# Threshold attention and a gated MLP on one core: for two of 32 head pairs, thresholds are subtracted by TensorE

## The chip, the cores and the metric

The kernel runs on one core of a Trainium2 chip. The metric is the device time of one execution in microseconds (us); the kernel before has a median of 1337.23 us over three runs (1337.0 to 1337.47). The engines of the core are called PE (TensorE), ACT (ScalarE), DVE (VectorE), POOL (GpSimd) and SP (SyncE).

## What is computed

```
q, k, v: (8, 8, 576, 64) float32        # batch, heads, sequence, head dim
scores = q @ k.T / 8
thresh = max(scores, last axis) - tau   # tau = 0.02
scores = where(scores >= thresh, scores, -1e9)
attn   = softmax(scores)                # sum + 1e-9
x      = (attn @ v) as (4608, 512)      # tokens by heads * head dim
h      = x @ w_in                       # 512 x 2048
out    = (h * sigmoid(1.702 * h)) @ w_out   # 2048 x 512
```

Everything is float32. The weights arrive as 64-bit floats and are converted on the chip.

## The kernel before

**Attention.** Two heads of a batch make a pair, so there are 32 pairs n, and four pairs make a batch of 576 tokens. Scores are kept transposed, keys on partitions: a pair has nine key tiles j of 64 keys (NK = 9), and a PSUM tile holds, for one j, both heads h and the two halves c of the queries, each in its own 64x64 quarter of the PE array. Two key tiles make an SBUF tile t of 128 x 1152 (four of them and a short last one of 576, so NKT = 4). The steps of a pair, with their line in the profile:

- load_qk and load_v (L356, L367): DMAs issued by SP; prep (L467): two DVE transposes, one each for q and k.
- scores_run (L483): PE, four matmuls of 64x288 for each j, into one of three PSUM places (psA).
- keep (L500): ACT copies the place to SBUF, 128 x 576, and frees it.
- in_groups (L506): DVE takes maxima per tile t through a transposing reduction; over_tiles (L515) and over_halves (L526, L530) finish the maximum of each query, less the threshold gap. over_halves joins the two key halves in four pieces of 32 partitions and then one step over all 128.
- The thresholds are spread over all partitions into a tile mb: by spread_max (L541), one DVE transpose, for pair 2 and from pair 8 on; for pairs 0, 1 and 3 to 7 (BY_DMA) by turn_rows (L536, L537), row_out (L550) and row_in (L559): DVE turns the row, SP sends it to DRAM and reads it back to 64 partitions at a time.
- sub (L564): DVE subtracts mb from the scores in place, five instructions a pair.
- mask (L570): ACT, Prelu with a slope of 1e30 for negative values, so that they become hugely negative; exps (L574): ACT, Exp.
- sums_by_pe and values (both L585): PE matmuls of the weights by ones (den) and by v (pv). Pairs 0 to 4 have their sums from PE (BY_PE = 5), later ones from DVE.
- one_row (L616), spread_sums (L640, L642) and place_x (L659): DVE makes the reciprocals and writes x, transposed, into the xT tiles.

Pairs 1 and 3 have their scores and transposed inputs in an area of their own (APART), which later serves the feed-forward.

**Weights.** load_w (POOL queue, L418, L419) brings 32 pieces of a weight, which DVE (cv_ex, cv_frac, cv_end: L429, L443, L447, L455) and ACT (cv_power, L437) convert. Pieces wait in two places in the arena and in four staging places inside w_out.

**Feed-forward.** The tokens are taken in 18 blocks of 256. The first two go through mm1_0 (PE, L714), tanh (ACT, L683), gelu_0 (DVE, L720) and mm2 (L696); later ones through mm1 (L674) or, for the last four, product1 (L779), and through product (L865), seven products in place of eight. mm1_0 of the first two blocks needs place_x of pairs 0 to 3, that is the whole first batch.

**What sets the order.** No queue order is written by hand. Each step is entered by task(...) with an engine, a cost in us, a rank, what it comes after, and the places that it takes and gives back. run_in_order then plays the tasks through with these costs: whenever an engine is free, it takes the ready task with the lowest rank whose places are free, and issues its instructions at that moment, so the play decides the order of each engine's queue. The rank of an attention step is its pair number plus a bias by the step's name, from EARLY for pairs 0 to 3, SECOND for pairs 4 to 7 and LATER for the rest; weights have ranks of their own (CV, W_RANK). On the chip each queue runs in that order and waits on semaphores.

Of the kernel before, what the change touches and what calls it, by code (L numbers as in the profile page):

```python
# [10 lines left out]
FP32 = mybir.dt.float32  # L11
# [8 lines left out]
P = 128  # L20
# [10 lines left out]
def kernel(  # L31
# [83 lines left out]
    stop = const.tile([P, 1], FP32, name="stop")  # L115
    shift = const.tile([P, 1], FP32, name="shift")
# [9 lines left out]
    for x in ("raw0", "raw1", "qkT0", "qkT1", "mb"):  # L126
# [6 lines left out]
        "exps": -13.03,  # L133
        "in_groups": 3.54,
        "keep": 8.7,
        "load_qk": -0.35,
        "load_v": 3.02,
        "mask": -4.3,
        "one_group": -16.49,
        "one_row": 10.29,  # L140
        "over_halves": 4.51,
        "over_tiles": -2.08,
        "place_x": -19.47,
        "prep": -10.76,
        "row_in": 6.33,
        "row_out": 13.15,
        "scores_run": 17.81,
        "spread_max": -2.62,
        "spread_sums": 6.57,
        "sub": 6.26,  # L150
        "sums_by_pe": 0.52,
        "turn_rows": -2.02,
        "values": 6.25,
        "w_sum": 2.08,
        "x_sum": -12.81,
    }
    SECOND = {
        "exps": -9.22,
        "in_groups": 17.42,
        "keep": 18.09,  # L160
        "load_qk": -6.19,
        "load_v": 2.25,
        "mask": -4.66,
        "one_group": 1.4,
        "one_row": -7.39,
        "over_halves": -5.63,
        "over_tiles": -0.54,
        "place_x": -17.43,
        "prep": 1.16,
        "row_in": -11.07,  # L170
        "row_out": -10.78,
        "scores_run": -2.82,
        "spread_max": 8.98,
        "spread_sums": 4.05,
        "sub": 6.07,
        "sums_by_pe": 26.56,
        "turn_rows": -2.56,
        "values": 3.27,
        "w_sum": -0.95,
        "x_sum": 0.01,  # L180
    }
    LATER = {
        "exps": 3.18,
        "in_groups": 6.02,
        "keep": 0.05,
        "load_qk": -5.33,
        "load_v": 3.86,
        "mask": 11.98,
        "one_group": -4.73,
        "one_row": -15.77,  # L190
        "over_halves": 0.98,
        "over_tiles": 0.3,
        "place_x": 4.38,
        "prep": 4.34,
        "row_in": 6.22,
        "row_out": 6.41,
        "scores_run": -12.36,
        "spread_max": -11.89,
        "spread_sums": -3.87,
        "sub": -1.6,  # L200
        "sums_by_pe": -3.04,
        "turn_rows": 14.13,
        "values": -6.55,
        "w_sum": 4.92,
        "x_sum": 4.0,
    }
    CV = {
        "cv_end": -9.13,
        "cv_ex": 4.45,
        "cv_frac": 2.56,  # L210
        "cv_power": -3.6,
        "load_w": -6.63,
# [4 lines left out]
    QUARTERS = ("scores", "scores_run", "values", "sums_by_pe")  # L217
# [76 lines left out]
    JOINT = 7  # L294

# [183 lines left out]
    def scores(n, j):  # L479
        ps = psA.tile([P, 2, 512], FP32, name="ps", tag="ps")  # L480
        for h in range(2):
            for c in range(2):
                nc.tensor.matmul(  # L483
                    ps[ts(c, KT), h, 0:SH],
                    lhsT=mats[n, 1][ts(h, D), ts(j, KT)], rhs=mats[n, 0][ts(h, D), ts(c, SH)],
                    start=True, stop=True,
                )
        if j == NK - 1:
            del mats[n, 0], mats[n, 1]
        pss[n, j] = ps  # L490
# [31 lines left out]
    def over_halves(n):  # L522
        r = stats[n, ALU.max]
        o = work.tile([P, QB], FP32, name="fold", tag="fold", bufs=1)
        for x in range(4):
            nc.vector.tensor_scalar(  # L526
                out=o[ts(x ^ 1, 32)], in0=r[ts(x, 32)], scalar1=gap[ts(x, 32)], scalar2=None,
                op0=ALU.subtract,
            )
        nc.vector.scalar_tensor_tensor(  # L530
            out=r, in0=r, scalar=gap, in1=o, op0=ALU.subtract, op1=ALU.max
        )

    def turn_rows(n):

        nc.vector.tensor_copy(out=flat[0][:, 0:QB], in_=stats[n, ALU.max])  # L536
        nc.vector.transpose(out=flat[1], in_=flat[0])  # L537

# [52 lines left out]
    def values(n, tiles):  # L591
        if 0 in tiles:
            pvs[n] = psA.tile([P, 2, 512], FP32, name="pv", tag="ps")
        v_m, pv = vs[n], pvs[n]
        by_values(n, lambda j, h: v_m[:, j, h, :], [pv[:, c, :] for c in range(2)], tiles)
        if n < NPAIR:
            free_scores(n, tiles)
# [304 lines left out]
    nc.gpsimd.memset(ones, 1.0)  # L902
    nc.gpsimd.dma_start(
# [26 lines left out]
    BY_PE = 5  # L930
# [7 lines left out]
    W_RANK = (16.81, 18.37, 9.14, 15.61, 0.39, 3.55)  # L938
# [211 lines left out]
    for n in range(NP):  # L1150
# [65 lines left out]
        else:  # L1216
            for js in [range(x, x + 3) for x in range(0, NK, 3)] if n >= WHOLE else [[x] for x in range(NK)]:
                new = sum((own(n, "s_m") if x < NK - 1 else ("s_t",) for x in js if x % 2 == 0), ())
                a = task(
                    "PE", 0.484 * slow * len(js), r, scores_run, n, js, after=[pq, pk] + after,  # L1220
                    take=("psA",) * len(js) + new,
                    give=own(n, "qkT0", "qkT1") if js[-1] == NK - 1 else (),
                )
                after = [a]
                for j in js:
                    copied(n, r, j, a)
        a = task("DVE", 0.35, r, over_tiles, n, ALU.max, after=mx)
        a = task("DVE", 1.05, r, over_halves, n, after=[a, tau_done])
        if n in BY_DMA:
            a = task("DVE", 0.4, r, turn_rows, n, after=[a], take=("row",))  # L1230
            a = task("SP", 0.6, r, row_out, n, after=[a], lag=3.3)
            m = task(
                "SP", 1.0, r, row_in, n, after=[a], take=own(n, "mb"), give=("row",),
                lag=5.2,
            )
        else:
            m = task("DVE", 0.78, r, spread_max, n, after=[a], take=own(n, "mb"))
        spread[n] = m
        ws, subs = [], [m]
        for t in range(NKT + 1):  # L1240
            tail = t == NKT
            a = task(
# [9 lines left out]
        if n < NPAIR:  # L1252

            pv = den = None
            for t in every:
                first = t == 0
                den = task(
                    "PE", (0.97 if t < NKT else 0.484) * slow, r, sums_by_pe, n, [t], True, after=[ws[t], den],
                    take=("psM", "psM") if first else (),
                )  # L1260
                pv = task(
                    "PE", (0.97 if t < NKT else 0.484) * slow, r, values, n, [t], after=[ws[t], den, pv, lv],
                    take=("psA",) if first else (), give=(back[t],) if t < NKT else ("s_t", v_m),
                )
            su = []
            a = task("DVE", 1.07, r, one_row, n, after=[den], give=("psM", "psM"))
        else:
# [3 lines left out]
            if n < BY_PE:  # L1271
                a = task("PE", 4.36, r, sums_by_pe, n, every, False, after=ws + [pv], take=("psA",), give=back)
                a = task("DVE", 1.07, r, one_row, n, after=[a], give=("psA",))
            else:
                su = [
                    task("DVE", 0.66 if t == NKT else 1.27, r, in_groups, n, t, ALU.add, after=[ws[t]])
                    for t in range(NKT + 1)
                ]
                a = task("DVE", 0.35, r, over_tiles, n, ALU.add, after=su + [pv], give=back)
                a = task("DVE", 1.6, r, one_group, n, after=[a])  # L1280
# [40 lines left out]
```

## Time and profile before

| What | Value |
|---|---|
| median of three runs | 1337.23 us |
| profiled execution, its own time | 1339.0 us |
| its span, first to last instruction | 1337.1 us |
| mean granted PE clock | 0.981 |
| PE busy | 1268.7 us (95%) |
| DVE busy | 1051.7 us (79%) |
| ACT busy | 646.0 us (48%) |
| POOL busy | 246.7 us (18%) |
| shares of the chain that ended last | PE 57%, DVE 26%, ACT 7%, issue 4%, DMA 4% |

The page of the profile cuts the span in 40 slices and gives the busy share of each engine in tenths. Groups of instructions are given by line, engine and operation, with the shape written and read, the count, busy time and mean of one. A float32 matmul of the program leaves two records, so the counts of PE in the profile are twice those of the code: 36 matmuls of scores for a pair are 72 records. The view of waits puts a wait down to the event that came last; the chain follows the work that ended last back from the end of the span; the timeline lists instructions in order of time, with the idle time ahead of them in brackets.

### The profile page before, as it was taken

What the parts mean: (1) busy time and instruction counts of PE and PEld (TensorE: products, weight loads), DVE (VectorE), ACT (ScalarE), POOL (GpSimd) and SP (SyncE); (2) the same over time, 40 slices, a digit from 0 to 9 for tenths busy, and PEclk for the clock granted to TensorE, in tenths of its full rate; (3) what the DMA queues carried; (4) which work ended last, traced back from release to release, by engine and by line L of the source; (5) the groups of instructions that cost most, each with busy time, mean ns of one, the idle gap of its engine ahead of it and who ended that gap; (6) DMA issues with size and microseconds to landing.
All of it is one profiled execution on the core that took longest, in us unless ns stands there. A gap on an engine that the chain in (4) does not pass through costs nothing.

```text
span 1337.1 us, 22553 instructions
## 1 busy us (share of the span) xinstructions
PE 1268.7 (95%) x9128; PEld 983.2 (74%) x9128; DVE 1051.7 (79%) x1720; ACT 646.0 (48%) x830; POOL 246.7 (18%) x290
## 2 busy tenths in 40 slices
PE   5739899899999999999999999999999999999998
PEld 2426774357777777777878777777777778888887
DVE  7899899899999888878788888878787892662642
ACT  4885473866565545555455554454555540210210
POOL 1012111002122120302121202121121216120120
PEclk8869999899999999999999999999999999999999
DMA  8597875545221212111212121211211010000000
GB/s 157 178 240 212 248 222 132 90 93 86 46 42 36 52 37 52 27 44 21 51 36 52 36 52 37 52 37 27 51 29 34 19 34 0 17 1 24 9 0 32
DMA packets 245473, 88.48 MB, mean 66 GB/s; under 512 B 229626, under 2 KB 233722, under 8 KB 245370
## 3 DMA queue, kind: packets, MB, share of 16 engines
q1 hardware_dynamic: 231642, 49.02, 18.4%
q0 software_dynamic: 11360, 37.74, 9.5%
q8 instruction: 71, 1.16, 0.3%
q10 hardware_dynamic: 2368, 0.30, 0.2%
q14 instruction: 32, 0.26, 0.1%
HBM read 73.36 MB, written 9.47 MB: 62 GB/s over the span
## 4 chain that ended last, share of the span: by engine, by line
PE 57%; DVE 26%; ACT 7%; issue 4%; DMA 4%; SPq 2%; DVEq 0%; ACTq 0%
PE ops L865 22%; PE hps L674 10%; PE pv L585 7%; PE ps L483 6%; DVE part L506 6%; DVE arena L564 6%; PE ps L779 4%; PE ps L865 4%; ACT arena L574 3%; PE ops L779 3%; DVE arena L686 2%; ACT arena L570 2%; DVE fold L526 2%; DVE arena L467 2%; ACT arena L500 1%
## 5 line engine op out<-in xcount | busy, mean ns | idle before, releaser
L506 DVE TRANSPOSE_TENSOR_REDUCE part<-arena 128x36 f32<-128x1152 f32 (+1 forms) x295 | 359.9, 1239 | 92.9 <-ACT arena L500 83.5
L674 PE MATMUL hps<-xT,w_in 128*128 128x256 f32 x1536 | 339.7, 381 | 2.7 <-DVE arena L686 2.6
L674 PEld LDWEIGHTS hps<-xT,w_in 128*128 128x128 f32 x1536 | 290.4, 190 | 51.0 <-DVE arena L686 7.0
L500 ACT COPY arena<-ps 128x576 f32<-128x576 f32 x288 | 171.2, 645 | 174.2 <-PE ps L483 174.1
L570 ACT ACTIVATE arena<-arena 128x1152 f32<-128x1152 f32 (+1 forms) x160 | 169.3, 1058 | 153.2 <-DVE arena L564 153.2
L483 PE MATMUL ps<-arena 64*64 64x288 f32 x2304 | 178.7, 424 | 41.1 <-ACT arena L574 16.8
L865 PE MATMUL ops<-w_out,arena 128*128 128x256 f32 x896 | 203.5, 382 | 4.0 <-DVE arena L686 4.0
L564 DVE TENSOR_TENSOR arena<-arena 128x1152 f32<-128x1152 f32 (+1 forms) x158 | 196.4, 1290 | 8.2 <-DMA arena<-row 7.7
L574 ACT ACTIVATE arena<-arena,shift,scl 128x1152 f32<-128x1152 f32 (+1 forms) x160 | 200.3, 1252 | 4.2
L865 PEld LDWEIGHTS ops<-w_out,arena 128*128 128x128 f32 x896 | 169.3, 190 | 32.6 <-DVE arena L686 7.8
L831 POOL TENSOR_TENSOR arena<-arena 128x256 f32<-128x256 f32 x56 | 51.9, 927 | 650.4 <-DVE arena L686 541.2
L483 PEld LDWEIGHTS ps<-arena 64*64 64x64 f32 x2304 | 86.9, 139 | 108.4 <-ACT arena L500 30.9
L585 PE MATMUL pv<-arena 64*64 64x288 f32 x2176 | 160.5, 409 | 0.0
L865 PE MATMUL ops<-arena 128*128 128x256 f32 x672 | 150.8, 381 | 0.0
L865 PEld LDWEIGHTS ops<-arena 128*128 128x128 f32 x672 | 127.5, 190 | 19.2 <-issue 2.2
L683 ACT ACTIVATE th<-hps 128x512 f32<-128x512 f32 x112 | 65.9, 588 | 134.3 <-PE hps L674 107.8
L585 PEld LDWEIGHTS pv<-arena 64*64 64x64 f32 x2176 | 82.6, 134 | 54.2 <-issue 12.5
L887 DVE SCALAR_TENSOR_TENSOR osb<-ops,osb 128x256 f32<-128x256 f32 x98 | 39.3, 413 | 59.1 <-PE ops L865 55.9
L686 DVE SCALAR_TENSOR_TENSOR arena<-th,hps 128x512 f32<-128x512 f32 x96 | 64.0, 667 | 24.0 <-ACT th L683 23.4
L714 PE MATMUL hps<-xT,w_in 128*128 128x256 f32 x256 | 58.6, 390 | 3.6 <-DVE arena L720 3.6
L714 PEld LDWEIGHTS hps<-xT,w_in 128*128 128x128 f32 x256 | 49.2, 195 | 13.1 <-DVE arena L720 4.4
L844 POOL TENSOR_TENSOR arena<-arena 128x512 f32<-128x512 f32 x28 | 35.6, 1270 | 115.1 <-PE ops L865 115.1
(110 smaller groups left out, 1107.3 us busy)
## 6 DMA issues: line engine op xcount, KB each, us to landing
arena<-in_v_dram SPq DMA_DIRECT2D x128, 144.0 KB, 3.3
arena<-in_q_dram SPq DMA_DIRECT2D x128, 72.0 KB, 3.1
out_dram<-osb SPq DMA_DIRECT2D x36, 256.0 KB, 2.0
arena<-in_k_dram SPq DMA_DIRECT2D x124, 72.0 KB, 2.5
w_out<-in_moe_w_in_dram POOLq DMA_DIRECT2D x12, 512.0 KB, 7.7
arena<-in_moe_w_out_dram POOLq DMA_DIRECT2D x12, 512.0 KB, 5.4
w_out<-in_moe_w_in_dram POOLq DMA_DIRECT2D x12, 511.6 KB, 9.3
arena<-in_moe_w_out_dram POOLq DMA_DIRECT2D x12, 511.6 KB, 6.2
```

The lines of the kernel that those rows point to most:

```text
L483: nc.tensor.matmul(ps[ts(c, KT), h, 0:SH], lhsT=mats[n, 1][ts(h, D), ts(j, KT)], rhs=mats[n, 0][ts(h, D), ts(c, SH)], start=True, stop=True,)
L500: nc.scalar.copy(out=sT[n, t][:, u], in_=pss.pop((n, j))[:, :, 0:SH])
L506: nc.vector.tensor_reduce(out=stats[n, op][:, t * 2 * QB : min(2 * t + 2, NK) * QB], in_=sT[n, t].rearrange("p u h (g d) -> p (u h g) d", ...
L564: nc.vector.tensor_tensor(out=s, in0=s, in1=mbs[n].unsqueeze(1).to_broadcast(list(s.shape)), op=ALU.subtract)
L570: nc.scalar.activation(out=s, in_=s, func=AF.Prelu, alpha=STEEP)
L574: nc.scalar.activation(out=s, in_=s, func=AF.Exp, scale=scl, bias=shift)
L585: nc.tensor.matmul(o[c][ts(h, D), 0:SH], lhsT=left(j, h)[ts(c, KT)], rhs=sT[n, t][ts(c, KT), u, h, :], start=(j == 0), stop=(j == NK - 1),)
L674: nc.tensor.matmul(hidden[j][:, ts(f, BLK)], lhsT=w_in[:, c, ds((f * HF + j) * P, P)], rhs=xTs[blk][:, c, :], start=(c == 0), stop=(c == N ...
L686: nc.vector.scalar_tensor_tensor(out=g[:, :, j, :], in0=two(ths.pop(j)), scalar=1.0, in1=two(hidden.pop(j)), op0=ALU.add, op1=ALU.mult,)
L714: nc.tensor.matmul(hidden[j][:, ts(i, BLK)], lhsT=w_in[:, c, ts(j, P)], rhs=xTs[i][:, c, :], start=(c == 0), stop=(c == NDC - 1),)
L779: nc.tensor.matmul(places[j, x], lhsT=left[:, c, ts(j, P)], rhs=right[:, c, :], start=(c == 0), stop=(c == 1),)
L865: nc.tensor.matmul(banks[blk][k][:, ts(o, HM)], lhsT=left[:, j, :], rhs=right[:, j, :], start=(j == 0), stop=(j == HF - 1),)
```

## The change

For the third and fourth pair (n = 2 and 3, TWICE) the subtraction on DVE goes. Their scores are computed, copied and reduced to maxima as before. over_halves then writes the thresholds straight into a small tile, in four pieces of 32 partitions in place of one step over 128 (and turn_rows' copy is not needed), and row_blocks transposes that tile and multiplies it by a constant pattern of ones and zeros (own_row), which gives, for each head, a block-diagonal arrangement of the thresholds, 128 x 288. again computes each key tile's scores a second time into PSUM and adds, in the same accumulation, four matmuls of a constant matrix of zeros and minus ones (minus) by that arrangement, so that PSUM holds scores less thresholds. mask_one applies Prelu to PSUM, one key tile at a time, and writes SBUF, over the first copy of the scores; exps runs as before. Pair 2 has no spread_max any more, and pair 3 no turn_rows, row_out and row_in. The transposed q and k of the two pairs are kept until their last again.

Two constants are filled at the start by POOL (a memset of each, and four memsets and four selects of 32 partitions). The tables EARLY, SECOND, LATER, CV and W_RANK get new numbers throughout. BY_PE = 5 becomes the list SUMS_BY_PE = (0, 1, 2, 3, 4), with the same pairs in it.

```diff
+    minus = const.tile([P, 2, KT], FP32, name="minus")
+    own_row = const.tile([P, QB // 2], FP32, name="own_row")
...
+    TWICE = (2, 3)
...
-        if j == NK - 1:
+        if j == NK - 1 and n not in TWICE:
             del mats[n, 0], mats[n, 1]
...
+        if n in TWICE:
+            for x, y in ((0, 0), (1, 2), (2, 1), (3, 3)):
+                nc.vector.scalar_tensor_tensor(
+                    out=flat[0][ts(y, 32), 0:QB], in0=r[ts(x, 32)], scalar=gap[ts(x, 32)],
+                    in1=o[ts(x, 32)], op0=ALU.subtract, op1=ALU.max,
+                )
+            return
         nc.vector.scalar_tensor_tensor(
             out=r, in0=r, scalar=gap, in1=o, op0=ALU.subtract, op1=ALU.max
         )
...
+    def row_blocks(n):
+        nc.vector.transpose(out=flat[1], in_=flat[0])
+        mb = home(n, "mb")[:, 0:SH]
+        nc.vector.tensor_tensor(
+            out=mb.rearrange("p (g i) -> p g i", i=32),
+            in0=flat[1].unsqueeze(1).to_broadcast([P, QB // 2, 32]),
+            in1=own_row.unsqueeze(2).to_broadcast([P, QB // 2, 32]), op=ALU.mult,
+        )
+        mbs[n] = mb
+
+    def again(n, j):
+        ps = psA.tile([P, 2, 512], FP32, name="ps", tag="ps")
+        for first in (True, False):
+            for h in range(2):
+                for c in range(2):
+                    if first:
+                        left = mats[n, 1][ts(h, D), ts(j, KT)]
+                        right = mats[n, 0][ts(h, D), ts(c, SH)]
+                    else:
+                        left, right = minus[ts(h, D), c, :], mbs[n][ts(h, D), :]
+                    nc.tensor.matmul(
+                        ps[ts(c, KT), h, 0:SH], lhsT=left, rhs=right, start=first, stop=not first,
+                    )
+        if j == NK - 1:
+            del mats[n, 0], mats[n, 1]
+        pss[n, j] = ps
+
+    def mask_one(n, j):
+        nc.scalar.activation(
+            out=sT[n, j // 2][:, j % 2], in_=pss.pop((n, j))[:, :, 0:SH], func=AF.Prelu, alpha=STEEP
+        )
...
+        if n in TWICE:
+            m = task("DVE", 0.6, r, row_blocks, n, after=[a], take=own(n, "mb"), give=("row",))
+        elif n in BY_DMA:
...
+            if n in TWICE:
+                for j in range(2 * t, min(2 * t + 2, NK)):
+                    m = task(
+                        "PE", 0.97 * slow, r, again, n, j, after=[m], take=("psA",),
+                        give=own(n, "qkT0", "qkT1", "mb") if j == NK - 1 else (),
+                    )
+                    a = task("ACT", 0.62, r, mask_one, n, j, after=[m] + mx, give=("psA",))
+                ws.append(task("ACT", 0.76 if tail else 1.24, r, exps, n, t, after=[a]))
+                continue
             a = task(
                 "DVE", 0.67 if tail else 1.35, r, sub, n, t, after=subs[-1:],
```

## The prediction

> **What bounds the kernel now.** I read the page first, for the shape of the span: in its part on slices TensorE (PE) has gaps in the first twelfth and is full afterwards, while VectorE (DVE) is full from the first microseconds on.
>
> ```profile
> PE   5739899899999999999999999999999999999998
> DVE  7899899899999888878788888878787892662642
> ```
>
> So I split the span where the feed-forward starts. The timeline of PE has the first feed-forward matmul (mm1_0, L714) at 124.25 us; the stages on both sides of that point give:
>
> ```profile
> 0.00:124.25 124.25, 77.58 (x992) 48.45 (x992) 105.92 (x185) 85.37 (x108) 18.75 (x42) 0.84 0.77 197
> 124.25:400.00 275.75, 263.19 (x1831) 179.03 (x1828) 259.47 (x424) 169.00 (x212) 42.15 (x56) 0.98 0.53 123
> 400.00:1337.00 937.00, 927.90 (x6311) 755.74 (x6309) 686.27 (x1113) 391.64 (x512) 185.76 (x192) 1.00 0.15 32
> ```
>
> The columns are the stretch, its length, busy time of PE, of PE's weight loads, DVE, ScalarE (ACT) and GpSimd, the granted clock, DMA. Before 124.25 us PE idles 46.7 us and DVE is busy 105.9; afterwards PE idles about 22 us of 1213. The start-up is DVE's, the rest is PE's. A change pays in the time at which the first feed-forward matmul can start, provided that it leaves PE no more work after it. The view of waits, start-up alone, then the timelines of DVE, ACT and PE around pairs 2 and 3 (the third and fourth):
>
> ```profile
> PE ps L483 <- ACT arena L574: 16.8, 1, 16.8
> PE den L585 <- ACT arena L574: 10.1, 2, 7.4
> ACT arena L570 <- DVE arena L564: 8.7, 2, 4.7
> ```
>
> ```profile
> 76.05 5.12 DVE L564 TENSOR_TENSOR arena<-arena 128x1152 f32<-128x1152 f32 x4
> 122.52 0.94 DVE L659 TENSOR_TENSOR xT<-pv,arena 128x256 f32<-128x256 f32 x4
> ```
>
> ```profile
> 77.39 1.16 ACT L570 ACTIVATE arena<-arena 128x1152 f32<-128x1152 f32 x1 [4.72 <-DVE arena L564]
> 99.06 0.87 ACT L574 ACTIVATE arena<-arena,shift,scl 128x576 f32<-128x576 f32 x1
> ```
>
> ```profile
> 88.75 2.20 PE L483 MATMUL ps<-arena 64*64 64x288 f32 x16 [16.84 <-ACT arena L574]
> 124.25 2.00 PE L714 MATMUL hps<-xT,w_in 128*128 128x256 f32 x8
> 210.73 1.15 PE L483 MATMUL ps<-arena 64*64 64x288 f32 x16
> 211.70 1.15 PE L585 MATMUL pv<-arena 64*64 64x288 f32 x16
> ```
>
> The reader is to see: DVE comes to pair 2's subtraction at 76.05, ACT masks and exponentiates pairs 2 and 3 without a hole from 77.39 to 99.93 (22.5 us), PE waits 16.8 us in one piece for it, then needs the rest up to 122.5, where pair 3's place_x frees the first feed-forward matmul.
>
> **What the Trainium skill says.** "TensorE: Matmul & The Clock Gate", What's actually happening: after an idle window of about 3.4 us the array runs at half clock until it has been busy for as long. The trace agrees: 16 records take 2.20 us after the idle stretch at 88.75, 1.15 us at 210.73. "ScalarE: Activation LUTs", What ACT_TABLE_LOAD costs: an activation with immediate operands takes 186 ns + 0.833 ns per element, and two in a row overlap by 93 ns: 666 and 573 ns for 576 elements. The trace agrees: copies of 576 out of PSUM (L500) take 0.64 us alone and 0.56 each in a row. "TensorEngine Tiling (Array Packing)", PSUM Bottleneck: tiling speeds the matmuls up, not the emptying of PSUM. That is the risk of this change, which fills three PSUM places twice as often. For one price I use "VectorE: DVE Perf Modes", the section on the TRN2 errata: (N + 151) / 0.96 ns for an fp32 tensor_tensor; the trace's 1344 ns for 1152 elements (page price 1357) agrees.
>
> **The change part by part.**
> DVE, removed: eight subs of 1152 at 1.29 us (20.6 / 16) = 10.3; two of 576 at 0.75 = 1.5; pair 2's spread_max 0.78; pair 3's turn_rows 0.18 + 0.21; the last step of over_halves, twice 0.24. Sum 13.4. Added: that step as four pieces of 32x18 each, eight at 0.225 (3.6 / 16, the fold row) = 1.8; two 128x32 transposes at 0.21; two 128x288 multiplications, which no row shows: the page prices 0.46, the place_x rows of 256 and 224 elements (0.413, 0.378) extend to 0.45. I take 0.45; even 0.8 each moves the sum by 0.7. Sum 3.1. Net -10.3 us.
> ACT: eight Prelus of 1152 at 1.15 and two of 576 at 0.67 (10.5) become eighteen of 576 out of PSUM. At 0.57 in a row they are 10.3, at 0.64 alone 11.6. I take 0: between -0.2 and +1.1.
> PE: each key tile's scores once more and the thresholds, eight matmuls where one pass has four. In the dense stretch eight matmuls (16 records) follow each other in 0.97 us (210.73 to 211.70), so 9 x 0.97 = 8.7 us a pair, 17.5 us for both; up to twice that at half clock.
> SyncE: pair 3's row goes no more through DRAM (two row_out and two row_in issues), and a DVE wait of 2.2 us for it at 86.6 goes. Against that, the new order puts four conversions of late weight pieces about 6 us behind the step that frees their staging places, while such a piece lands 7.7 to 9.3 us after its issue: a new wait of 2 to 3 us. I set the two against each other. Pair 1's v (2.65 us of issue) now goes ahead of pair 2's q and k, which DVE takes up only at about 25: 0. GpSimd: ten small memsets and selects at the start, ahead of tau's load, which is used at 9.2; 0.
> Waits that the change adds: an again waits for one of three PSUM places, which ACT's mask_one frees; behind it in PE's queue stand the den and pv matmuls of the same pair and pair 4's scores, for which one_row and place_x wait on DVE. Pair 2's transposed q and k are held until its last again, so pair 4's two prep steps on DVE come after it.
>
> The built program tells what moved. On both sides of the change 16 key tiles of pairs 4 and 5 are scored ahead of the first feed-forward matmul, and what PE has to do after it is the same, matmul for matmul in number and kind. So the 17.5 us lie wholly ahead of it, in the 46.7 us of idle, and the end moves as that matmul moves, but for waits further on. Three bounds on its new time:
> (1) DVE's queue. Work up to pair 3's place_x falls by 10.3; one reduction of pair 4 (1.3) moves behind it, and about 2.0 of weight conversion moves ahead of it: -9.6. DVE idles 16 us before 124.25 now, mostly waiting for the first loads and for pair 1's thresholds from DRAM (45.19); those stay, within 2 us, and the wait that goes pays for the one that comes. That gives 124.25 - 9.6 = 114.7.
> (2) ACT. Ahead of pair 2's thresholds DVE has 55.1 us of queue, where it had 65.3 up to the end of the first sub: 10.2 less, so the thresholds are there at about 67, the first score 1 us later. ACT is not free then: pair 3's nine copies, moved ahead of it, run to about 70. From there the 22.5 us of both pairs, plus four weight activations and three copies now between them (4.5), end at 97. It then takes PE the last sums (0.5), 72 values matmuls (8.7) and eight key tiles (3.9): 110 to 111.
> (3) PE. From the first again to the first feed-forward matmul stand 352 matmuls (144 again, 72 den, 72 pv, 64 scores): at 0.121 each 42.7 us. From 69.5 that gives 112.2 without a hole, and about 2 more for each idle stretch long enough to lose the clock.
> DVE ends last, with PE two microseconds behind: I take 114, a shift of -10.2 us. After it PE's waits stay: the largest now are 7.8 us for score places (L500), 4.0 and 2.6 for the activations of later blocks, 3.6 for mm1_0's. DVE's work between feed-forward steps falls behind PE's by up to 12.8 us in the old order and 12.1 in the new, so nothing there should grow; I count 0, between -4 and +5, since the new ranks reorder pairs 4 to 10 by microseconds.
> The profiled execution took 1339.0 us with a span of 1337.1; the median of the runs is 1337.23, nearly the span. A span of 1337.1 - 10.2 = 1326.9 reads as 1327.0 in the median.
>
> **The rivals.**
> A. As worked out: 1327.0, with 1322 to 1331.5 around it. For it: DVE full in the start-up, and equal work after it.
> B. PE and the PSUM places take DVE's place: three more holes at about 2 us of lost clock each, so the first feed-forward matmul comes at 120 and the gain is about 4: 1333. For it: bounds 1 and 3 are within 3 us. Against: an again of two tiles and its share of den are 2.9 us of PE against 2.5 of ACT, so PE hardly idles.
> C. Slower, by one mechanism: the stretch of 42.7 us of PE runs at half clock, because each again waits for an activation and never lets PE be busy long enough. Today the granted clock between 77 and 100 us is 0.52. The point from which it decides is a mean clock of 0.78, where 42.7 / 0.78 = 54.7 us from 69.5 just reach 124.25; at 0.70 it is 61 us, the first matmul at 130.5 and the end at 1343.5. Against: today's 0.52 goes with PE idle for 14.4 us of those 23.
> D. More: the later waits shrink as well (DVE's peak lag falls, the score places' 4.7 us wait goes): 1321.
> That the change doesn't do what it says is no case: the built program has eight long and two short subs fewer and 144 matmuls more.
>
> **How the numbers follow.** A 0.60, D 0.07, B 0.18, C 0.15. Below 0.2% (2.7 us, about what a measurement of this kernel can tell from no change) lie B's end (0.05) and C's start (0.02): same 0.07. Faster 0.60 + 0.07 + 0.13 = 0.80, slower 0.13. The range reaches from D's 1320 to B's end at 1336, leaving out C and a bit of D, about 0.18.
>
> **What would show it.** In the changed kernel's profile: first L714-type matmul near 114; DVE 10 us less busy, PE about 17 more; pair 2's first Prelu near 70, ACT done with pair 3 near 97; PE's clock above 0.9 between 70 and 112; idle after the first feed-forward matmul still about 22 us. Wrong if that matmul comes before 110 or after 119, if PE's waits for activations in the again stretch pass 6 us, or if idle after it changes by over 5.

## The result, and the profile after

| | before | after |
|---|---|---|
| median, us | 1337.35 (1337.00 to 1340.06, 4 runs) | 1323.20 (1322.92 to 1325.37, 4 runs) |
| profiled execution: own time, span, us | 1339.0, 1337.1 | 1322.9, 1321.1 |
| mean granted clock of PE | 0.981 | 0.994 |
| busy PE, DVE, ACT, us | 1268.7, 1051.7, 646.0 | 1275.5, 1040.9, 644.9 |

The ratio after to before is 0.9891, 95% interval 0.9876 to 0.9905: the changed kernel is 14 us faster, inside the predicted range and 4 us below the predicted 1327.0. The spans of the two profiled executions differ by 16.0 us, which is more, since the one before lies 1.65 us above its median; the stages below add up to the 16.0.

On the page, the slices of PE and DVE. PE's gap in the third slice is closed:

```profile
PE   4798999999999999999999999999999999999998
DVE  7979999999998988878787888888787791652642
```

The stages on both sides of the first feed-forward matmul, which stood at 124.25 us and stands at 119.72 (columns as in the prediction):

```profile
0.00:119.72 119.72, 89.18 (x1280) 55.91 (x1280) 98.65 (x186) 84.65 (x116) 20.55 (x52) 0.93 0.82 203
119.72:400.00 280.28, 274.85 (x2002) 188.41 (x2000) 270.18 (x438) 179.31 (x227) 48.62 (x62) 1.00 0.51 121
400.00:1321.00 921.00, 911.44 (x6142) 742.46 (x6138) 672.08 (x1093) 380.99 (x497) 182.33 (x186) 1.00 0.15 33
```

Only 4.5 of the 16.0 us come ahead of that matmul; 11.5 come after it. The same table, cut at the first mm1_0, the first mm2 and the first mm1 matmul, before and then after:

```profile
124.25:199.22 74.97, 71.37 (x468) 56.99 (x465) 68.55 (x118) 44.13 (x57) 15.19 (x28) 0.98 0.78 233
199.22:291.44 92.22, 87.15 (x586) 41.45 (x585) 84.62 (x139) 55.90 (x71) 5.30 (x6) 0.96 0.48 101
291.44:1337.10 1045.66, 1032.57 (x7089) 836.34 (x7087) 792.57 (x1281) 460.61 (x597) 207.42 (x214) 1.00 0.17 36
```

```profile
119.72:187.64 67.92, 67.86 (x445) 54.98 (x441) 66.42 (x113) 42.06 (x54) 15.10 (x28) 1.00 0.80 242
187.64:277.63 89.99, 86.98 (x608) 41.19 (x609) 85.85 (x141) 59.46 (x75) 5.32 (x6) 1.00 0.53 113
277.63:1321.10 1043.47, 1031.45 (x7089) 834.70 (x7087) 789.99 (x1279) 458.77 (x596) 210.54 (x214) 1.00 0.17 36
```

The stages gain 7.1, 2.2 and 2.2 us. In the first of them PE has no idle left (67.86 of 67.92) where it had 3.6 us, and its clock is full.

The timeline of ACT (first and last activation of pairs 2 and 3), of DVE (pair 3's place_x) and of PE after the change:

```profile
69.44 0.65 ACT L587 ACTIVATE arena<-ps 128x576 f32<-128x576 f32 x1 [0.31 <-PE ps L579]
95.79 0.87 ACT L626 ACTIVATE arena<-arena,shift,scl 128x576 f32<-128x576 f32 x1
```

```profile
116.88 0.95 DVE L711 TENSOR_TENSOR xT<-pv,arena 128x256 f32<-128x256 f32 x4 [0.73 <-PE pv L637]
```

```profile
119.72 1.99 PE L766 MATMUL hps<-xT,w_in 128*128 128x256 f32 x8
```

ACT starts and ends with the two pairs where the prediction put it (70 and 97). The waits of PE from 68 to 119.7 us:

```profile
PE ps L495 <- DVE arena L479: 3.7, 1, 3.7
PE ps L495 <- ACT arena L512: 1.2, 1, 1.2
PE ps L579 <- ACT arena L587: 0.6, 2, 0.3
```

The second scores wait 0.6 us for their places in all. The long wait is for a transpose of pair 5's keys. PE's busy time, clock, DMA share and GB/s in three parts of this stretch:

```profile
68.09:94.00 25.91, 24.15 (x388) 1.00 0.64 226
94.00:110.20 16.20, 16.20 (x264) 1.00 0.95 256
110.20:119.72 9.52, 5.78 (x67) 0.82 0.98 217
```

### The profile page after: what moved, and what is told of

It reads as the page before. It is cut to its first block, busy times and chain, and to the rows that moved or that the text cites. A ratio compares the mean times of both kernels' runs of the same rounds, so it can differ in the third digit from the quotient of the medians.

```text
span 1321.1 us, 23139 instructions
## 1 busy us (share of the span) xinstructions
PE 1275.5 (97%) x9416; PEld 986.8 (75%) x9416; DVE 1040.9 (79%) x1717; ACT 644.9 (49%) x838; POOL 251.5 (19%) x300
## 4 chain that ended last, share of the span: by engine, by line
PE 61%; DVE 21%; ACT 10%; issue 4%; DMA 3%; SPq 0%; POOL 0%; DVEq 0%; ACTq 0%
PE ops L917 22%; PE hps L726 12%; PE ps L495 8%; PE pv L637 7%; DVE part L518 6%; DVE arena L616 5%; PE ps L831 4%; PE ps L917 4%; ACT arena L626 4%; ACT arena L622 3%; PE ops L831 3%; DVE arena L738 2%; DVE fold L538 2%; ACT arena L512 1%; DVE arena L479 1%
## 5 line engine op out<-in xcount | busy, mean ns | idle before, releaser
L518 DVE TRANSPOSE_TENSOR_REDUCE part<-arena 128x36 f32<-128x1152 f32 x295 | 359.6, 1239 | 92.3 <-ACT arena L512 82.4
L726 PEld LDWEIGHTS hps<-xT,w_in 128*128 128x128 f32 x1536 | 289.7, 190 | 50.8 <-DVE arena L738 6.0
L622 ACT ACTIVATE arena<-arena 128x1152 f32<-128x1152 f32 (+1 forms) x150 | 158.8, 1059 | 138.6 <-DVE arena L616 138.5
L495 PE MATMUL ps<-arena 64*64 64x288 f32 x2304 | 175.4, 420 | 30.0 <-DVE arena L479 12.1
L616 DVE TENSOR_TENSOR arena<-arena 128x1152 f32<-128x1152 f32 (+1 forms) x149 | 186.6, 1293 | 0.5
L917 PEld LDWEIGHTS ops<-arena 128*128 128x128 f32 x672 | 127.2, 190 | 19.5 <-issue 2.2
L735 ACT ACTIVATE th<-hps 128x512 f32<-128x512 f32 x112 | 65.8, 587 | 136.7 <-PE hps L726 112.2
L748 PE MATMUL ops<-w_out,arena 128*128 128x512 f32 x128 | 56.5, 597 | 0.1
```

The source lines that it names most:

```text
L495: nc.tensor.matmul(ps[ts(c, KT), h, 0:SH], lhsT=mats[n, 1][ts(h, D), ts(j, KT)], rhs=mats[n, 0][ts(h, D), ts(c, SH)], start=True, stop=True,)
L518: nc.vector.tensor_reduce(out=stats[n, op][:, t * 2 * QB : min(2 * t + 2, NK) * QB], in_=sT[n, t].rearrange("p u h (g d) -> p (u h g) d", ...
L616: nc.vector.tensor_tensor(out=s, in0=s, in1=mbs[n].unsqueeze(1).to_broadcast(list(s.shape)), op=ALU.subtract)
L622: nc.scalar.activation(out=s, in_=s, func=AF.Prelu, alpha=STEEP)
L726: nc.tensor.matmul(hidden[j][:, ts(f, BLK)], lhsT=w_in[:, c, ds((f * HF + j) * P, P)], rhs=xTs[blk][:, c, :], start=(c == 0), stop=(c == N ...
L735: nc.scalar.activation(out=ths[j], in_=hidden[j], func=AF.Tanh, scale=GELU_SCALE / 2)
```

## The experiments

All were compared with the kernel before, run beside them on their chip (its medians there lie between 1338.45 and 1338.84 us; beside the change it was 1337.35). Spans and stages come from one profiled execution each, and this can lie some us off the median of its runs: those of structure and k6_short lie 5.0 and 3.5 us below, that of again_ranks 4.0 above. So a stage says something where several traces agree. "Old order" is that of the kernel before, "new order" that of the changed one. The first table gives the measured ratio with its 95% interval, the second the stages of the span in us: up to the first mm1_0, from there to the first mm2, to the first mm1, to the end.

| run | median, us | ratio to before |
|---|---|---|
| the change | 1323.20 | 0.9891 (0.9876 to 0.9905) |
| ranks | 1385.22 | 1.0340 (1.0318 to 1.0361) |
| structure | 1340.91 | 1.0012 (0.9989 to 1.0035) |
| no_sub | 1340.16 | 1.0005 (0.9991 to 1.0019) |
| no_row | 1336.05 | 0.9980 (0.9964 to 0.9996) |
| no_sub_no_row | 1336.81 | 0.9985 (0.9975 to 0.9995) |
| own_ranks | 1338.00 | 0.9996 (0.9986 to 1.0007) |
| k6_short | 1334.53 | 0.9968 (0.9955 to 0.9981) |
| dve_early | 1333.59 | 0.9965 (0.9951 to 0.9979) |
| dve_back | 1334.26 | 0.9958 (0.9942 to 0.9974) |
| again_more | 1326.61 | 0.9914 (0.9895 to 0.9933) |
| again_one | 1327.79 | 0.9916 (0.9901 to 0.9930) |
| again_ranks | 1324.60 | 0.9881 (0.9851 to 0.9910) |

| run | to mm1_0 | to mm2 | to mm1 | to the end | span |
|---|---|---|---|---|---|
| before | 124.3 | 75.0 | 92.2 | 1045.7 | 1337.1 |
| no_sub | 125.5 | 75.5 | 90.9 | 1045.7 | 1337.6 |
| no_row | 123.9 | 74.6 | 92.3 | 1046.0 | 1336.8 |
| no_sub_no_row | 123.1 | 74.6 | 92.4 | 1046.0 | 1336.1 |
| k6_short | 121.9 | 70.0 | 91.5 | 1045.7 | 1329.1 |
| the change | 119.7 | 67.9 | 90.0 | 1043.5 | 1321.1 |
| dve_early | 131.7 | 67.9 | 90.0 | 1043.4 | 1333.0 |
| dve_back | 121.2 | 76.1 | 91.1 | 1043.5 | 1331.9 |
| again_more | 121.6 | 67.8 | 91.8 | 1043.5 | 1324.7 |
| again_one | 120.9 | 67.8 | 93.2 | 1043.4 | 1325.3 |
| ranks | 112.2 | 116.1 | 112.2 | 1042.6 | 1383.1 |
| structure | 129.0 | 89.0 | 73.1 | 1043.1 | 1334.2 |
| own_ranks | 129.7 | 71.1 | 89.4 | 1045.5 | 1335.7 |
| again_ranks | 124.6 | 71.0 | 92.6 | 1038.6 | 1326.8 |

The theories at the start were T1 (DVE sets the pace up to about 330 us, on both sides of the first mm1_0), R1 (my prediction's picture: the start-up is DVE's, the rest PE's) and R2 (the new ranks alone bring the gain). T2 to T6 came as runs spoke against these; each is stated in the expectation of the run that tests it.

### Ranks without structure, and structure without ranks

**ranks.** The kernel before with the change's numbers in four of the five tables (SECOND stays old); for example

```diff
     CV = {
-        "cv_end": -9.13,
+        "cv_end": 2.48,
...
-        "load_w": -6.63,
+        "load_w": -39.98,
```

> The kernel before with the new ranks in four of the five tables (EARLY, LATER, CV and the weights' ranks; SECOND stays old) and no second computation of scores. Theory T1 (VectorE sets the pace of the first 330 us on both sides of the first mm1_0, so the end moves by what VectorE loses in work and in idle time there): its work is unchanged at 1051.7 us, so the time stays near that of before, 1333 to 1342, and what it gains is VectorE idle time. Rival R2 (the new order alone makes the gain): 1323 to 1328. Rival R1 (the end moves as the first mm1_0 matmul moves, all after it belongs to TensorE): 1337 less whatever that matmul moves.

1385.22 us, 47 us slower; no theory expected that. With the old operations these ranks bring the first mm1_0 at 112 us and then make it wait: PE waits 21.3 us in one piece for the weights' conversion (w_in) and 23.5 us for w_out. R2 falls for this set of ranks. It says nothing of other sets, and the change's own five tables together were not tried on the old operations.

**structure.** The changed kernel, with four of the five tables taken back; LATER stays new, and the three new steps have no bias in the others.

> The changed kernel with the old ranks in four of the five tables (EARLY, SECOND, CV and the weights' ranks; LATER stays new; the three new tasks have no bias). T1: VectorE's work is 10.3 us less as in the changed kernel, its idle time in the first 330 us is not tuned away, so 1324 to 1331, with most of the gain kept. R2: within 3 us of before, 1334 to 1340. R1: 1337 less the shift of the first mm1_0 matmul.

1340.91 us, no faster than before, where T1 wanted most of the gain; R2's "within 3 us of before" came true here, though ranks speaks against R2. The runs scatter widely (1333 to 1348). In the trace DVE has 10.9 us less (1040.8), but up to 330 us it waits 10.8 us for rows from DRAM (7.7 before), and 4.6 us in one piece for PE. So less DVE work in this order isn't enough either: the two parts of the change work together. What the tail of the table shows: every run with the change's LATER ranks takes 1042.6 to 1043.5 us from the first mm1 to the end, every run with the old ones 1045.7 to 1046.0. These 2.2 us belong to LATER.

### DVE's work taken away in the old order

**no_sub.**

```diff
         s = sT[n, t].rearrange("p u h s -> p u (h s)")
+        m = mbs[n]
+        if n in (2, 3):
+            s, m = s[:, :, 0:16], m[:, 0:16]
         nc.vector.tensor_tensor(
-            out=s, in0=s, in1=mbs[n].unsqueeze(1).to_broadcast(list(s.shape)), op=ALU.subtract
+            out=s, in0=s, in1=m.unsqueeze(1).to_broadcast(list(s.shape)), op=ALU.subtract
         )
```

> The kernel before, its order of instructions unchanged, with the ten subtractions of pairs 2 and 3 cut to 16 of 576 columns (most of those scores keep their thresholds unsubtracted: that part of the computation is left out). VectorE loses 2 x (4 x 1.35 + 0.71) = 12.2 us and keeps ten operations of some 0.2 us, so 10.3 us net, just the changed kernel's balance, without TensorE's second scores and without new ranks. T1: 1325 to 1328, the gain partly ahead of the first mm1_0 and partly after it. R1: the end moves exactly as the first mm1_0 moves. R2: 1334 or more. If TensorE's places or its 17.5 us cost the changed kernel anything, this one is faster than it by that much.

1340.16 us: nothing gained with 10.2 us less of DVE (1041.5), and R1's and T1's step "so much less DVE work, so much earlier" is wrong for the old order (R2's "1334 or more" held). DVE's timeline shows where the time went:

```profile
92.06 0.19 DVE L567 TENSOR_TENSOR arena<-arena 128x32 f32<-128x32 f32 x1 [11.88 <-DMA arena<-row]
```

DVE waits 11.9 us for pair 3's thresholds to come back from DRAM, where it waited 2.2 before. The row doesn't just keep its time, it is there 5.5 us later: at 92.1 and not at 86.6. The queue of SP, then that of POOL, in the kernel before:

```profile
82.92 1.13 SPq L559 DMA_DIRECT2D arena<-row  x2
```

```profile
84.31 0.53 POOL L418 DMA_DIRECT2D w_out<-in_moe_w_in_dram  x1 [11.96 <-ACT arena L570]
```

and without the subtractions:

```profile
82.69 2.33 SPq L559 DMA_DIRECT2D arena<-row  x2
```

```profile
80.12 0.53 POOL L418 DMA_DIRECT2D w_out<-in_moe_w_in_dram  x1 [7.56 <-ACT arena L573]
```

Before, the row was issued ahead of a burst of eight weight loads, and DVE had it 3.6 us later. Without the subtractions ACT is earlier, so POOL's weight loads start 4.2 us earlier; five of the eight now stand ahead of the row, which takes 9.4 us. As the traces read, the faster engine triggered the transfers that it then waited for; no run held the loads back to show it.

From this came T2 (the row's trip and DVE's work hide each other, both must go), T3 (the trip alone is what counts) and T4 (neither counts in the old order).

**no_row.** Pair 3's four row DMAs left out, its thresholds read from what lies in their place:

```diff
     def row_out(n):
+        if n == 3:
+            return
...
         mb = home(n, "mb")
+        if n == 3:
+            mbs[n] = mb
+            return
```

> The kernel before, its order on VectorE, ScalarE and TensorE unchanged, without pair 3's trip of the threshold row through DRAM (four DMAs on SP; pair 3 subtracts the values that lie in its place from pair 1, so that part of the computation is left out). VectorE's work is unchanged. T2 (the trip and VectorE's other work hide each other, so each must go for either to be worth anything; the run without the subtractions waited 11.9 us for this row): the wait of 2.2 us goes, 1334 to 1338. T3 (the trip through SP's queue alone sets this stage): 1325 to 1330. T1 (VectorE's work alone): 1336 to 1339.

1336.05 us, 0.2% less, inside the ranges of both T2 and T1, and not as T3 had it.

**no_sub_no_row.** Both edits together.

> Both at once in the kernel before: the ten subtractions of pairs 2 and 3 cut to 16 of 576 columns, and pair 3's row not taken through DRAM (both parts of the computation are left out). The order is still that of before, no score is computed twice, no new ranks. T2: VectorE's 10.3 us now show, 1325 to 1329. T3: the same as without the row alone. T4 (neither is worth anything in the old order; the new order is what brings it): 1335 to 1339.

1336.81 us, no more than the row alone. T2 falls and T4 stands: in the old order DVE's 10 us and the row together are worth 0.05 to 0.25%. DVE now waits for the next things in that order, for pair 4's queries and for a weight's step on ACT:

```profile
82.69 0.78 DVE L467 STREAM_TRANSPOSE arena<-arena 128x576 f32<-128x576 f32 x1 [4.80 <-DMA arena<-in_q_dram]
100.81 2.02 DVE L455 SCALAR_TENSOR_TENSOR w_in<-w_out 128x512 f32<-128x512 int32 x3 [4.11 <-ACT w_out L437]
```

And ACT begins pair 2's mask at 77.6, as before (77.4), since the subtractions come after that point in the old order; the changed kernel has it at 69.4. From there to 100.0 ACT is busy 22.1 of 22.4 us (before, 22.2 of 22.5), and DVE 12.7 where it was 19.5: most of the subtractions stood beside ACT's work, which takes as long without them. So the old order has no use for the time that DVE gets back.

### DVE's work put back in the new order

**dve_early** and **dve_back.** An idle reduction of 512 elements, in the first run twice after each group reduction of pairs 2 and 3, in the second once after each gelu_0:

```diff
+    spent = const.tile([P, 8], FP32, name="spent")
+
+    def spend():
+        nc.vector.tensor_reduce(
+            out=spent, in_=ones.unsqueeze(1).to_broadcast([P, 8, D]), axis=AXL.X, op=ALU.max
+        )
...
+        if n in (2, 3) and op == ALU.max:
+            for _ in range(2):
+                spend()
```

> The changed kernel, order unchanged, with two idle VectorE reductions of 512 elements (about 0.6 us each) after each of the ten group reductions of pairs 2 and 3, so about 12 us of VectorE work before 72 us, ahead of the first mm1_0, about as much as the change takes out of that stage. If VectorE sets the pace there: 1331 to 1336. If the start-up waits for something else (weights, 8.8 us of VectorE waits between 45 and 117 us): 1323 to 1328.

> The changed kernel, order unchanged, with one idle VectorE reduction of 512 elements (about 0.6 us) after each of the 16 gelu_0, so about 10 us of VectorE work between 127 and 191 us, all after the first mm1_0. T1: the end goes back by most of that, 1329 to 1334. R1 and any theory in which TensorE is the bound after the first mm1_0: 1323 to 1325, because VectorE has over 200 us of idle time in the whole.

DVE's busy time rose by 12.2 and 9.1 us, the spans by 11.9 and 10.8, and by the ratios to before the times rose by 9.9 and 9.0. (The first set ended at 83 us, not 72, as it delays itself.) In the new order most of DVE's work lies on the path, ahead of the first mm1_0 (131.7 against 119.7) and after it (the stage to mm2 grows by 8.2). R1 falls: after the first mm1_0 PE is the busier engine, but added work of DVE still makes that stage longer. T1 holds, for the new order only.

dve_early also separates the two parts of the change, roughly, since its added work stands at other places than the subtractions did: it is the new order with as much DVE work as before, and 0.35% (0.21 to 0.49%) or 4.7 us faster than before. Its first mm1_0 is 7.4 us later than before's, as the new order lets it be, and its three later stages are as short as the changed kernel's, to 0.1 us.

### TensorE's second scores, more and less

**again_more** issues each second score matmul once more (8.7 us of PE).

```diff
-        for first in (True, False):
+        for first, once in ((True, True), (True, False), (False, False)):
...
-                        ps[ts(c, KT), h, 0:SH], lhsT=left, rhs=right, start=first, stop=not first,
+                        ps[ts(c, KT), h, 0:SH], lhsT=left, rhs=right, start=first, stop=once or not first,
```

> The changed kernel, order unchanged, with the four score matmuls of each of the 18 second computations issued once more (72 matmuls at 0.1213 us, so 8.7 us more of TensorE work in pairs 2 and 3, ahead of the first mm1_0). If TensorE's added work is covered, as the prediction had it: 1322 to 1326. If TensorE sets that stage: 1329 to 1333.

1326.61 us, just past the range for "covered": the ratio is 0.0023 above the change's (3 us), with intervals that overlap, the span 3.6 us longer, half of it (1.9 us) ahead of the first mm1_0.

**again_one** computes only the first of the nine pieces a second time.

```diff
     def again(n, j):
+        if j:
+            if j == NK - 1:
+                del mats[n, 0], mats[n, 1]
+            return
```

with mask_one in place for the others.

> The changed kernel, order unchanged, in which only the first of the nine pieces of pairs 2 and 3 is computed a second time; the other sixteen Prelus work in place on the scores without subtraction (that part of the computation is left out). TensorE loses 16 x 8 x 0.1213 = 15.5 us of work ahead of the first mm1_0 and has a gap again between 70 and 89 us. If that work is merely covered: 1321 to 1324. If it is a cost (the doubled one cost 3.5 us for 8.7): 1314 to 1320. T5 (the second scores keep TensorE busy and so at full clock when the sums of pair 2 begin, where the kernel before ran at half): 1325 to 1332, slower with less work.

1327.79 us: 15.5 us less of PE's work, and not faster but slower than the change, by 4.2 us of span. All four runs of it lie above all four of the change, though the ratios' intervals overlap by a hair (0.9901 and 0.9905). T5 was the one that expected this sign. PE's busy time, clock, DMA share and GB/s in two stretches of 10 us, of this run:

```profile
80.00:90.00 10.00, 4.49 (x40) 0.57 1.01 376
90.00:100.00 10.00, 6.84 (x69) 0.58 1.04 371
```

and of the changed kernel:

```profile
80.00:90.00 10.00, 9.43 (x156) 1.00 1.00 373
90.00:100.00 10.00, 8.81 (x141) 1.00 1.10 335
```

The second scores keep the clock full, as T5 says: with them 32 records of pair 2's sums take 2.12 us (88.66), in no_sub_no_row, after PE's gap, 3.96. And PE's busy time in the whole falls by 7.3 us (1268.2 against 1275.5), not by 15.5, as what is left runs slower.

But this makes little of the difference at the end. The first mm1_0 is only 1.2 us later without them. The other 3.2 us appear between the first mm2 and the first mm1, and there the traces name another cause: DVE waits for a pair's row from DRAM, and then PE for ACT's copies. DVE and PE in again_one, then PE in the changed kernel, where DVE has no such wait:

```profile
238.33 5.83 DVE L624 TENSOR_TENSOR arena<-arena 128x1152 f32<-128x1152 f32 x5 [1.96 <-DMA arena<-row]
```

```profile
250.64 1.26 PE L495 MATMUL ps<-arena 64*64 64x288 f32 x16 [3.78 <-ACT arena L512]
```

```profile
247.46 1.26 PE L495 MATMUL ps<-arena 64*64 64x288 f32 x16 [1.69 <-ACT arena L512]
```

again_more, which has more of PE's work and not less, has the same two waits (1.63 and 3.46 us) and is 1.8 us longer in this stage. So the clock is shown, but that it decides the end is not: the traces put 3.2 of the 4.2 us down to the late row. Whether that row is late because of the edits or by chance is open.

"TensorE: Matmul & The Clock Gate", What's actually happening, in the Trainium skill, says that half clock comes after an idle window of about 3.4 us, and that the window is free-running. Here less was enough: in again_one a gap of 2.80 us sufficed for half clock (16 records in 2.20 us at 71.59).

### Single late arrivals, and other orders

**k6_short.** One load of the kernel before cut to an eighteenth:

```diff
+                c = 1 if n == 6 and which else SH // 16
                 queue.dma_start(
-                    out=blocks[ds(64 * h + 32 * j, 32), :, :],
-                    in_=src[b, 2 * hp + h, :, ts(j, 32)].rearrange("(c p) d -> p c d", p=32),
+                    out=blocks[ds(64 * h + 32 * j, 32), 0:c, :],
+                    in_=src[b, 2 * hp + h, 0 : 32 * c, ts(j, 32)].rearrange(
+                        "(c p) d -> p c d", p=32
+                    ),
```

The waits in the kernel before, on DVE and then on PE:

```profile
157.25 0.78 DVE L467 STREAM_TRANSPOSE arena<-arena 128x576 f32<-128x576 f32 x1 [3.38 <-DMA arena<-in_k_dram]
```

```profile
160.66 12.20 PE L714 MATMUL hps<-xT,w_in 128*128 128x256 f32 x48 [3.60 <-DVE arena L720]
```

48 records take 12.20 us after the gap; the changed kernel's 152 in 33.07 us are 0.2176 each, which makes 10.4 for 48. So the wait costs 3.6 and the clock after it 1.8 us.

> The kernel before, order unchanged, in which the load of pair 6's keys brings one eighteenth of its rows (the rest of that pair's keys are left out). VectorE waited 3.4 us for this load at 157 us, TensorE then 3.6 us for a gelu_0, and ran at a lower clock after it. T6 (what the changed kernel gains after the first mm1_0 comes from such single late arrivals, which another order avoids): the wait goes and the end comes 3 to 6 us earlier, 1331 to 1335. If VectorE's wait is covered by something else: 1336 to 1339.

1334.53 us, 0.32% (0.19 to 0.45%) less, as T6 expected. The stage from mm1_0 to mm2, with PE idle 0.1 us of it:

```profile
121.90:191.90 70.00, 69.88 (x468) 55.53 (x464) 67.89 (x118) 43.49 (x57) 15.25 (x28) 1.00 0.77 238
```

That is 5.0 of the 7.1 us that the changed kernel gains in this stage. The wait that goes is in all four other traces with the old order's tables (2.7 to 3.6 us); the edit also takes away that load's traffic, which was not tried apart. 23 records fewer in the stage (468 and 445; 24 of scores take 1.69 us in a row) are most of the rest. The 2.4 us ahead of the stage can't be the edit's, since the load comes at 142 us; the other four traces lie between 123.1 and 125.5 us there, and this one is that of the fastest of ten runs.

**own_ranks.** The kernel before with all five tables new, picked so that its own play (run_in_order) ends 6.2 us earlier.

> The kernel before, all of its operations, with ranks of its own, found anew for it with its own rule of what may run when; no score is computed twice. R2 (an order is what pays, the second scores are only one way to have another one): 1320 to 1328. T6 (the order pays only together with the work that the second scores take from VectorE, since the old work leaves no better order): 1332 to 1339.

1338.00 us, no gain. The play's 6.2 us did not come: the first mm1_0 is 5.4 us later than before, with PE waiting 14.1 us in one piece for DVE's one_row, and DVE 7.0 us for a load of keys. This speaks for T6, as far as one other order can.

**again_ranks.** The changed kernel with ranks picked in the same way; its play ends 6.6 us earlier.

> The changed kernel, all of its operations, with ranks found anew for it in the same way as those of the run with ranks of its own for the kernel before; by the rule's own costs and due times it ends 6.6 us sooner than the changed kernel (that of the kernel before with its own new ranks was promised 6.2 us and got none). If the rule's costs hold where VectorE sets the pace: 1314 to 1320, faster than both kernels. If loads and the clock, which the rule does not price, decide: 1321 to 1332.

1324.60 us, not to be told from the change (0.9881 and 0.9891, intervals overlapping). From the first mm1 to the end it takes 1038.6 us, 4.9 less than the change, and up to there it loses 10.6 us, in a profiled execution that was the slowest of the four. The change's order up to the first mm1 with this tail was not tried.

## Why the prediction was right, and where it failed

The time lies in the predicted range, but two of the three signs that I had named for being wrong came: the first mm1_0 came after 119 (119.72), and PE's idle time after it changed by more than 5 us (6.7). Only the waits for activations in the stretch of the second scores stayed small. The predicted shift was 10.2 us ahead of the first mm1_0 and nothing after it; measured were 4.5 and 11.5. That these two misses partly cancel is luck.

- **DVE, -10.3 us of work.** Right: 10.8 measured. That it shortens the path was right in the new order (12.2 us put back cost 11.9 of span, 9.9 by the ratios) and wrong as an argument: I drew it from the profile of before, and in that order the same work is worth 0.05 to 0.25%, row included.
- **ACT, 0.** Right: -1.1 us. Its first Prelu at 69.44, its end with pair 3 at 96.66, where I had 70 and 97.
- **PE, +17.5 us wholly in idle time.** Right for the second scores: 26 us from the first again on with 24.15 busy, and 0.6 us of waits for places. But PE as a whole is 6.8 us busier and not 17, since its other matmuls took less time. I counted no gain from the clock; again_one shows that it is the second scores that hold it at 1.00 from 80 to 100 us, where before had 0.50 and 0.55.
- **SP and POOL, 0.** Mis-sized: the row's wait of 2.2 us went, but DVE waits for weight pieces, in DMA or in their step on ACT, for 6.6 us up to 119.7 (2.7, 1.8, 1.2, 0.7 and 0.2), not 2 to 3.
- **The first mm1_0 at 114, DVE ending last.** Failed: 119.72, and PE's queue ended last. Pair 3's place_x is done at 117.8, and PE works on scores until 119.7. Bound (3) had 42.7 us of PE from the first again to that matmul without a hole, and it took 51.6: 5.5 us are waits (3.7 of them for pair 5's keys), and half of the other 3.4 is the lower clock after that wait (67 records in 5.78 us, at 0.0605 each 4.1). Bound (1) was off as well: DVE's work ahead of the matmul is 7.3 us less (105.92 and 98.65), not 9.6, since the new order moves more work ahead, and its idle time there is 2.7 us more (18.3 and 21.1), where I had none. DVE still sets the pace behind PE's waits, as dve_early shows.
- **"0, between -4 and +5" for all that follows.** The step that failed most: -11.5 us. PE's idle time after the first mm1_0 fell from 21.7 to 15.0 us, its busy time by 4.8. I took PE's 98% there for a bound that does not move. Its two largest waits, 3.6 us for a gelu_0 and 4.7 for score places, each had time at a lower clock behind it (0.66 from 160 to 165 us, 0.50 from 260 to 265). In the stage to mm2, 5.0 of 7.1 us are the load of pair 6's keys; to the end, 2.2 are the LATER ranks. Of the 2.2 us between mm2 and mm1 the score places are a part: that wait is 4.3 to 4.7 us in all five traces with the old order's tables, and 1.7 in the change, dve_early and dve_back; but with 3.5 and 3.8 us in again_more and again_one the stage is as long as in the old order.
- **The sum.** By dve_early the order is worth 4.1 us of span and DVE's saving 11.9 (4.7 and 9.9 by the ratios, each to some 2 or 3 us); the total was predicted as 10.2 + 0. So the 10.2 is about what the work is worth, though not where I placed it, and what I missed is the order's own 4 to 5 us. The milestone was at fault: a new order shifts work across the first mm1_0, so its time tells little of the end.
- **The rivals.** B's time for the first mm1_0 (120) came true, and PE did end last, but by one hole for pair 5's keys and not by the PSUM places. C, half clock, was the reverse: the clock rose. D, that later waits shrink, was right in kind, with the very wait for score places that it names, and its 1321 is nearer to the 1323.2 than A's 1327; I gave it 0.07.

What stays open: what makes the row late in again_one and again_more; how much of the order's gain is due to single arrivals that fall well in it; and if a still other order would do for the old operations what own_ranks did not.

## What to carry to other kernels

Here work taken off the engine that looked full paid only in an order that could use it: take it away alone first, as a run that leaves it out, and look at which wait comes in its place. Where an order is set by ranks, as here, don't judge by one milestone, since a new order moves work across it; compare stages, over more than one trace, and put the saved work back as idle operations to price it. An engine at 98% is not a bound if the 2% are waits for another one; here a wait of 3.6 us cost 1.8 us more at a lower clock after it.

## What the runs showed of the hardware

- Two DMAs that read a row of 2.3 KB to 64 partitions each were there 3.6 us after the first issue ahead of a burst of eight weight loads, and after 9.4 us in the midst of it (no_sub).
- A TensorE gap of 3.6 us cost 1.8 us more at lower clock; in again_one gaps of 2.8 and 2.7 us in a sparse stretch were followed by half speed (16 records in 2.20 us, where dense ones take 1.15, and 8 in 1.24, where they take 0.67).
- Prelu from PSUM over 128x576 took 0.65 us alone and 1.17 for two, no more than in SBUF (1.16 for 1152), and a DVE multiplication of two broadcast operands over 128x288 took 0.46, where those of 256 and 224 elements (0.413 and 0.378) extend to 0.45.
